# A log-space scan for the turned units, seven products for one more pair, and a new order of steps

## The chip, the cores and the metric

The kernel runs on one core of a Trainium2 chip. A core has a matrix engine (PE, with its weight loads shown apart as PEld), three engines for elementwise work (DVE, ACT and POOL), a queue engine (SP) that issues most transfers, and 16 DMA engines behind it. Each engine works through its own instructions in order and waits on semaphores for the others. The metric is the time of one execution on the device in microseconds, as the median of several executions.

## The reference

Two blocks follow one another, for 4 batches of 768 positions. In the first, 8 heads of 48 channels each keep a 48 x 48 state that decays per channel:

```python
f = 1.0 / (1.0 + np.exp(-f_logit))
for t in range(S):
    state = f[:, :, t, :, None] * state + np.einsum('bhd,bhe->bhde', k[:, :, t], v[:, :, t])
    y[:, :, t] = np.einsum('bhd,bhde->bhe', q[:, :, t], state)
```

The heads' outputs side by side are x, of 768 x 384 per batch. The second block mixes positions through a rank of 32 and channels through a hidden layer of 1536:

```python
h = xt @ U @ V                  # xt: x with positions last
u = x + h.transpose(0, 2, 1)
ch = np.maximum(u @ w_ch1, 0.0) @ w_ch2
out = u + ch
```

## The kernel before

**Units.** Two heads of one batch are a unit; there are 16, numbered 0 to 15, four per batch. A unit's 768 positions are cut into 12 chunks of 64. For a unit the kernel needs, per channel and position, the decay from a position to its chunk's end (the tile `late`, called X) and the inverse decay from the chunk's start (called Y). The keys are multiplied by X and the queries by Y. Then PE makes five groups of small products: `kept` (turns the scaled keys, tile pt), `states` (each chunk's contribution, tile ds), `scores` (within a chunk, tile sc), `read` (queries against the state, tile y) and `inner` (scores against v, added to the same y). A scan on DVE (L1111) carries the state from chunk to chunk.

**Three ways to X and Y.** Units 0 to 3 take the logarithm of the decay on ACT, sum it with a matrix product and take the exponential. Units 4 and 5 turn f on PE, take a sigmoid on ACT (`gates`, L923) and run two multiplying scans on DVE, one backwards for X (`keep`, L936) and one forwards for Y (`read`, L954, called `read_back` in the order of steps), with four small DVE instructions between them (L941 to L946). Units 6 to 15 (from `TURNED` on) do the same, but f, k and q are loaded in blocks and turned by DVE (L814), and the sigmoid is L931.

**The mixer.** For each batch, `low_rank`, `added_up` and `mix` make u; `turn` turns it (tile uT); then three pairs of position blocks go through the hidden layer. The first layer, `ch1`, makes six products per pair (tile pz, L339), each followed by a relu on ACT (L374). The second layer of batch 0, `ch2`, multiplies a pair in eight quarters (tile po, L394). The batches after it use `seven`: seven products of half the width in place of eight (tile pw, L428), by sums of blocks of w_ch2 that `quarters` makes once (four DVE subtractions, L610 to L613) and sums of the hidden layer's blocks (`sums_of`, four DVE instructions per pair). Batches 2 and 3 use `fewer` for the first layer: 15 products in place of 18, by sums of rows of w_ch1 (tile pp, L536).

**The weights.** The 24 blocks of w_ch1 and w_ch2 arrive as doubles. Each is loaded raw (L97), split by two ACT instructions (`halves`, L106 and L107), rounded by three DVE instructions (`join`, L113 to L115) and put together by one POOL addition (L116). From the seventh block on the raw data go into four buffers (`RAW`), so a load waits until a block loaded earlier has been joined.

**What sets the order.** PE's order is the program's in the whole kernel. From the start until the first two `ch1` products of batch 1, DVE's and ACT's are too, and SP's until `written.close()`. In this first part the order is that of the code: `steps` gives out the pieces of the attention, `Fill` puts pieces of the mixer between them, each weight's `end` follows a `ch1` product. After it, the pieces are collected in a list and run in the order of `ORDER2`, which permutes their 243 numbers; there a scheduler orders the engines other than PE.

**Memory between engines.** PE's results go to five PSUM tiles: three of two banks (`ps_big`: transposes, ds, sc, y, mixer sums) and two of one bank (`ps_mm`: pz, po, most pw). A tile is taken again when its last reader is done.

Of the kernel before, what the change touches and what calls it, by code (L numbers as in the profile page):

```python
# [18 lines left out]
WP = 384  # L19

RAW = 4
# [4 lines left out]

ORDER2 = (
# [44 lines left out]
SIGNS = (1, -1, 1, 1, 1, 1)  # L72


def weight_loader(nc, pool, dma):
# [8 lines left out]
    def load(dst, w, place=None):  # L84
# [25 lines left out]
        def join():  # L110
            y, r, hi = T["parts"]
            f = y.bitcast(F32)
            nc.vector.tensor_scalar(f, f, SMALLEST, LARGEST, ALU.max, ALU.min)  # L113
# [4 lines left out]
        def end():  # L118
            halves()
            join()  # L120
# [17 lines left out]
def RUN(piece):  # L138
    if TODO is None:
        return piece()  # L140
    TODO.extend(getattr(piece, "parts", (piece,)))


def of_parts(*parts):
    def run():
        for f in parts:
            f()

    run.parts = [p for f in parts for p in getattr(f, "parts", (f,))]
    return run  # L150
# [44 lines left out]
class Mixer:  # L195
# [6 lines left out]
    def __init__(self, tc, b, x, U, V, w1, w2, sums, ident, blocks, out, two, three, zp, ps_big, ps_mm, wide=False,  # L202
# [23 lines left out]
        def low_rank():  # L226
            pm = ps_mm.tile([P, 512], F32, name="ph", tag="mm")

            products_with_u(pm, slice(0, DM))
            h[0] = two.tile([P, DM], F32, name="h", bufs=2)  # L230
            nc.scalar.copy(h[0], pm[:, 0:DM])

        def added_up():

            pm = ps_mm.tile([P, 512], F32, name="ph", tag="mm")
            nc.tensor.matmul(pm[:, 0:DM], lhsT=blocks, rhs=h[0], start=True, stop=True)
            h[1] = two.tile([P, DM], F32, name="h", bufs=2)
            nc.scalar.copy(h[1], pm[:, 0:DM])
# [8 lines left out]
        def mix(t):  # L247

            s = t % 2
            if s == 0:  # L250
                pu[0] = ps_big.tile([P, 2, 512], F32, name="pu", tag="big")
            g = slice((t % NG) * R, (t % NG + 1) * R)
            nc.tensor.matmul(pu[0][:, s, 0:DM], lhsT=V[g, t // NG, :], rhs=h[1][g, :], start=True, stop=True)
            if s == 1:
                add(x[:, t - 1 : t + 1, :], x[:, t - 1 : t + 1, :], pu[0][:, :, 0:DM], ALU.add)


# [4 lines left out]
        def mix_four():  # L262
            big = ps_big.tile([P, 2, 512], F32, name="pu", tag="big")
# [4 lines left out]
            for t in range(2, NG):  # L268
                add(x[:, t, :], x[:, t, :], pms[t][:, 0:DM], ALU.add)
# [1498 lines left out]
```

## Time and profile before

| | us |
|---|---|
| median of 3 runs | 465.59 (465.1 to 465.73) |
| the profiled execution's own time | 465.49 |
| its span | 463.8 |
| PE busy | 454.1 |
| PE weight loads busy | 394.9 |
| DVE busy | 363.0 |
| ACT busy | 171.9 |
| POOL busy | 49.5 |

The span runs from the first to the last instruction of one execution; 1.7 us of the execution's time lie around it. An engine's busy time is the time in which at least one of its instructions runs. Matmuls overlap one another, and the profile models their ends, so PE can be shown busy while it works below its full pace; the starts of its instructions show the pace. A matrix product in float32 appears as two instructions. Lines such as L339 are lines of the kernel.

### The profile page before, as it was taken

What the parts mean: (1) busy time and instruction counts of PE and PEld (TensorE: products, weight loads), DVE (VectorE), ACT (ScalarE), POOL (GpSimd) and SP (SyncE); (2) the same over time, 40 slices, a digit from 0 to 9 for tenths busy, and PEclk for the clock granted to TensorE, in tenths of its full rate; (3) what the DMA queues carried; (4) which work ended last, traced back from release to release, by engine and by line L of the source; (5) the groups of instructions that cost most, each with busy time, mean ns of one, the idle gap of its engine ahead of it and who ended that gap; (6) DMA issues with size and microseconds to landing.
All of it is one profiled execution on the core that took longest, in us unless ns stands there. A gap on an engine that the chain in (4) does not pass through costs nothing.

```text
span 463.8 us, 13155 instructions
## 1 busy us (share of the span) xinstructions
PE 454.1 (98%) x5687; PEld 394.9 (85%) x5687; DVE 363.0 (78%) x614; ACT 171.9 (37%) x325; POOL 49.5 (11%) x58
## 2 busy tenths in 40 slices
PE   8999999999999999999999999999999999999997
PEld 5876888876666578899988889999989999999996
DVE  6668688988999689677799895879797974878652
ACT  6765776644332135234413542241212311212200
POOL 2002345544110101011000000000000000000000
PEclk9999999999999999999999999999999999999999
DMA  9948997678778814662406100000000100000001
GB/s 193 191 106 211 228 205 175 157 132 111 111 113 120 127 21 55 90 90 28 86 1 112 29 3 11 29 1 1 17 19 1 36 0 18 18 1 35 1 35 40
DMA packets 148584, 34.37 MB, mean 74 GB/s; under 512 B 136934, under 2 KB 146982, under 8 KB 148518
## 3 DMA queue, kind: packets, MB, share of 16 engines
q1 hardware_dynamic: 147718, 33.29, 37.2%
q8 instruction: 47, 0.77, 0.7%
q10 hardware_dynamic: 800, 0.15, 0.2%
q14 instruction: 19, 0.16, 0.1%
HBM read 28.70 MB, written 4.72 MB: 72 GB/s over the span
## 4 chain that ended last, share of the span: by engine, by line
PE 84%; DVE 7%; SPq 2%; ACT 2%; issue 2%; DMA 2%; POOL 0%; DVEq 0%; ACTq 0%; POOLq 0%
PE pw L428 27%; PE pz L339 18%; PE pp L536 18%; PE po L394 5%; PE y L1129 2%; SPq L721 2%; PE sc L1035 2%; PE y L1147 2%; PE ds L1086 2%; PE pt L1062 1%; DVE late L936 1%; PE put L327 1%; PE pt L837 1%; PE pt L895 1%; DMA w<-in_q_dram 1%
## 5 line engine op out<-in xcount | busy, mean ns | idle before, releaser
L339 PE MATMUL pz<-uT,w 128*128 128x256 f32 x420 | 96.4, 383 | 0.1
L339 PEld LDWEIGHTS pz<-uT,w 128*128 128x128 f32 x420 | 77.9, 190 | 10.9 <-ACT uT L328 0.3
L428 PE MATMUL pw<-w,z_all 128*128 128x192 f32 x216 | 37.7, 328 | 0.0
L428 PE MATMUL pw<-zw,w_raw 128*128 128x192 f32 x216 | 37.6, 328 | 0.0
L428 PEld LDWEIGHTS pw<-w,z_all 128*128 128x128 f32 x216 | 35.1, 190 | 0.9 <-DVE qT L243 0.5
L428 PEld LDWEIGHTS pw<-zw,w_raw 128*128 128x128 f32 x216 | 35.2, 190 | 0.5 <-issue 0.3
L116 POOL TENSOR_TENSOR w<-w_y,w_r 128x384 int32<-128x384 int32 x24 | 31.5, 1312 | 36.9 <-DVE w_y L115 22.5
L526 ACT ACTIVATE other<-other 128x512 f32<-128x512 f32 x18 | 11.4, 631 | 44.2 <-DVE other L243 44.2
L526 ACT ACTIVATE z_all<-z_all 128x512 f32<-128x512 f32 x18 | 11.3, 630 | 40.4 <-DVE z_all L243 40.4
L936 DVE TENSOR_TENSOR_SCAN late<-fz,late 128x768 f32<-128x768 f32 x12 | 21.1, 1754 | 6.6 <-ACT fz L931 6.5
L374 ACT ACTIVATE z_all<-pz 128x512 f32<-128x512 f32 x27 | 16.1, 597 | 26.9 <-PE pz L339 26.5
L394 PE MATMUL po<-w,zw 128*128 128x384 f32 x72 | 25.1, 495 | 0.0
L394 PE MATMUL po<-w,z_all 128*128 128x384 f32 x72 | 24.7, 493 | 0.0
L536 PE MATMUL pp<-v_nat,late 128*128 128x128 f32 x168 | 21.6, 276 | 0.0
L394 PEld LDWEIGHTS po<-w,zw 128*128 128x128 f32 x72 | 13.2, 190 | 9.6 <-issue 0.8
L1117 POOL COPY st<-added 128x576 f32<-128x576 f32 x8 | 12.5, 1560 | 81.0 <-DVE added L1111 64.6
L954 DVE TENSOR_TENSOR_SCAN late<-fz,other 128x768 f32<-128x768 f32 x12 | 21.0, 1748 | 0.1
L394 PEld LDWEIGHTS po<-w,z_all 128*128 128x128 f32 x72 | 13.3, 190 | 8.9 <-DVE o L243 0.6
L536 PEld LDWEIGHTS pp<-v_nat,late 128*128 128x128 f32 x168 | 20.2, 192 | 0.1
L1094 ACT COPY added<-ds 48x576 f32<-48x576 f32 (+2 forms) x29 | 17.8, 619 | 5.8 <-PE ds L1086 5.4
L536 PE MATMUL pp<-uT,late 128*128 128x128 f32 x144 | 19.3, 277 | 0.0
L113 DVE TENSOR_SCALAR w_y<-w_y 128x384 f32<-128x384 f32 (+3 forms) x27 | 12.1, 448 | 8.9 <-ACT w_y L106 8.9
(219 smaller groups left out, 908.4 us busy)
## 6 DMA issues: line engine op xcount, KB each, us to landing
w_raw<-in_moe_w_ch_dram SPq DMA_DIRECT2D x18, 384.0 KB, 3.8
out_dram<-o SPq DMA_DIRECT2D x17, 192.0 KB, 1.9
v_nat<-in_v_dram SPq DMA_DIRECT2D x16, 144.0 KB, 3.5
v_nat<-in_v_dram SPq DMA_DIRECT2D x32, 72.0 KB, 3.6
zw<-in_moe_w_ch_dram SPq DMA_DIRECT2D x6, 384.0 KB, 4.5
out_dram<-o SPq DMA_DIRECT2D x14, 96.0 KB, 2.2
w<-in_k_dram SPq DMA_DIRECT2D x4, 288.0 KB, 3.9
w<-in_q_dram SPq DMA_DIRECT2D x4, 288.0 KB, 4.3
```

The costliest lines, as they stand in the source:

```text
L113: nc.vector.tensor_scalar(f, f, SMALLEST, LARGEST, ALU.max, ALU.min)
L116: nc.gpsimd.tensor_tensor(dst.bitcast(I32), shaped(y.bitcast(I32)), shaped(r), ALU.add)
L339: nc.tensor.matmul(pm[:, i * 2 * P : (i + 1) * 2 * P], lhsT=w1[:, m, o : o + P], rhs=uT[a][:, m, :], start=(m == 0), stop=(m == NDC - 1))
L374: nc.scalar.activation(z[a, c][:, k : k + 2, :].rearrange("p i t -> p (i t)"), pm, AF.Relu)
L394: nc.tensor.matmul(pm, lhsT=z[a, i // NI][:, i % NI, s * P : (s + 1) * P], rhs=w2[:, i, :], start=(i == 0), stop=(i == NFC - 1))
L428: nc.tensor.matmul(W["pm"][:, n * HM : (n + 1) * HM], lhsT=lhs[:, i, :], rhs=rhs[:, i, :], start=(i == 0), stop=(i == NI - 1))
L526: nc.scalar.activation(dst, dst, AF.Relu, scale=float(SIGNS[n]))
L536: nc.tensor.matmul(pm[:, i, r * P : (r + 1) * P], lhsT=room["w"](wn)[:, r * P : (r + 1) * P], rhs=x_node(a, xn), start=((xn, wn) == of[0]) ...
L936: nc.vector.tensor_tensor_scan(backwards(X, S - 1, S), backwards(f, S, S), backwards(ends, S - 1, S), 0.0, ALU.mult, ALU.add,)
L954: nc.vector.tensor_tensor_scan(Y, f[:, 0:S], starts, 0.0, ALU.mult, ALU.add)
L1094: nc.scalar.copy(added[r, 1:].rearrange("p (e c s) -> p e c s", c=NBL, s=2)[:, e], ds[r, :, 0 : NBL * D].rearrange("p s (c e) -> p e c s", ...
L1117: nc.gpsimd.tensor_copy(st, states.rearrange(by_e, c=NCH))
```

## The change

There are three parts.

**Units 6 to 15 in logarithms.** `TURNED` units no longer use a sigmoid. POOL limits the raw f from below (`bound`), DVE turns it straight into `fz` (`gates`), ACT takes the exponential and then the logarithm of one plus it, both in one function table (`logs`), one backward scan on DVE sums the logarithms within each chunk (`keep`), and three ACT exponentials give X and the chunk's whole decay (`decay`) and Y (`read_back`). The second scan and the four small DVE instructions are gone for these units. Unit 6 has a third load of ACT's function table before it. Outside units 4 and 5 the copy into `wholes` (L917, L946) goes, since `least` holds the same numbers; `whole` is one constant tile whose first column stays zero.

**The first batch's third pair by `seven`.** The eight `ch2` quarters of pair 2 of batch 0 become seven half-width products with their sums. The four sums of w_ch2 are made earlier, between the products of pairs 0 and 1; the third of them goes into rows of `late` that the units no longer need, in two instructions. Two tiles instead of three are taken for these sums; the freed one holds two of the later sums of w_ch1.

**The order of steps.** Each piece is cut into named parts (a product `p`, the copy or sum that follows it, each transfer), and the first part of the kernel is run in the order of a table of names, `ORDER`, of 524 parts. Up to `close` it keeps the order that the code had. `ORDER2` is replaced by a permutation of 430 parts.

```diff
+        def bound_all():
...
+            nc.gpsimd.tensor_single_scalar(r["f"], r["f"], FLOOR, ALU.max)
+
+        def logs_of(i):
+            g = f[:, 0:S]
+            if i == 0:
+                if n == TURNED:
+                    nc.scalar.preload_act_table_set("natural_log_exp_and_others")
+                nc.scalar.activation(g, g, AF.Exp, scale=-1.0)
+            else:
+                nc.scalar.activation(g, g, AF.Ln, bias=1.0)
+
+        def log_scan():
+            g = f[:, 0:S]
+            nc.vector.tensor_tensor_scan(
+                backwards(g, S - 1, S), backwards(starts, S - 1, S), backwards(g, S - 1, S), 0.0, ALU.mult, ALU.add,
+            )
+
+        def decay_x():
+            X, g = late[:, 4, :], f[:, 0:S]
+            T["X"] = X
+            nc.scalar.activation(by_chunk(X)[:, :, 0 : C - 1], by_chunk(g)[:, :, 1:C], AF.Exp, scale=-1.0)
...
         def read():
             Y = T["Y"] = late[:, 5, :]
+            if n >= TURNED:
+                nc.scalar.activation(by_chunk(Y)[:, :, 0 : C - 1], by_chunk(f[:, 0:S])[:, :, 1:C], AF.Exp)
+                return
             nc.vector.tensor_tensor_scan(Y, f[:, 0:S], starts, 0.0, ALU.mult, ALU.add)
...
         def second(a):
-            if sums is None:
-                return [(2 * NFC * DM // NQ, lambda s=s, n=n: ch2(a, s, n)) for s in range(2) for n in range(NQ)]
...
+            if sums is None or wide and a < NA - 1:
+                return [(2 * NFC * DM // NQ, ch2(a, s, n)) for s in range(2) for n in range(NQ)]
```

Three stretches of `ORDER` of which the prediction speaks (names of weights, `end_w`, carry the block's number; `.t` and `.p` are products on PE):

```diff
+c.10 c.11 c.12 end_w6.halves end_w6.join load_w18 tb.m0.t load_w21 tb.m0.o end_w7.halves m0.t end_w7.join m0.o
+load_w17 c.02 m0.ch1.1.0p m0.ch1.1.0r end_w8.halves m0.ch1.2.0p end_w8.join fz1b load_w20 end_w9.halves fz0b
...
+read_back4 m0.ch1.2.2p m0.ch1.1.2r end_w15.halves queries4.f end_w15.join keys4.f m0.ch1.2.2r kept4.t
+m0.ch1.0.3p end_w16.halves end_w17.halves end_w17.join end_w16.join gates5.t m0.ch1.1.3p m0.ch1.0.3r gates5.s
+gates5.f keys5.t m0.ch1.2.3p m0.ch1.1.3r end_w18.halves kept4.o kept4.s queries4.m end_w19.halves end_w18.join
...
+m0.sv.2.01p queries9.f keys9.m scan8.s0 m0.sv.2.0e keys9.f m1.p m0.sv.2.10p m1.o m1.p#2 m1.o#2 m1.p2 logs10.e
```

More of the change, by code (lines that the diff above doesn't have):

```diff
@@ L279, in __init__ @@
+        mix_four = of_parts(("p4", mix_four_p), *[(f"f{t}", lambda t=t: mix_four_a(t)) for t in [0] + list(range(2, NG))])
+        first = 0
+        todo = []
+        if b > 1 and sums is not None:
+            todo += mix_four.parts
+            first = NG
+        for t in range(first, NCH):
+            todo += mix(t)
+        mix_blocks = of_parts(*todo)
         hs, last = {}, {}
         def low_rank_of(cols):
-            pm = ps_mm.tile([P, 512], F32, name="ph", tag="mm")
-            products_with_u(pm, cols)
@@ L284, in low_rank_of, with products @@
[L284 to L292 removed]
+            t = {}
+            def products():
+                t["pm"] = ps_mm.tile([P, 512], F32, name="ph", tag="mm")
+                products_with_u(t["pm"], cols)
@@ new lines, in put, with put_all, lo, lw @@
+        def put(label, piece):
+            todo.extend(tagged(label, piece).parts)
+        def put_all(pieces):
+            for piece in pieces:
+                RUN(piece)
+        def lo(n, *names):
+            load(n, *names)
+        def lw(i):
+            put(f"load_w{i}", weights[i][0])
+        for i in range(3):
+            put(f"busy{i}", lambda: busy(1))
+        put_all(front(0, "gates", "unpack_k", "unpack_q", "read_back", "keep"))
+        lo(1, "k", "q")
+        lo(2, "f")
@@ L1329, in factored_path @@
[L1329 to L1340 removed]
+        for i in range(FIRST, FIRST + 4):
+            lw(early + i)
```

825 lines of the change are left out of this document (505 added, 320 removed), and 31 rows, old and new, of the table ORDER2.

## The prediction

> **What bounds the kernel now.** I read the busy times first, then PE's by stage.
>
> ```profile
> PE 454.1 (98%) x5687; PEld 394.9 (85%) x5687; DVE 363.0 (78%) x614; ACT 171.9 (37%) x325; POOL 49.5 (11%) x58
> ```
>
> ```profile
> 20.00:40.00 20.00, 17.25 (x542) 14.27 (x532) 13.42 (x27) 13.44 (x35) 1.49 (x3) 1.00 0.53 139
> 80.00:100.00 20.00, 20.00 (x196) 17.20 (x196) 19.03 (x30) 12.04 (x24) 11.33 (x8) 1.00 0.71 159
> 120.00:140.00 20.00, 19.77 (x352) 13.01 (x351) 18.86 (x25) 7.42 (x13) 2.43 (x2) 1.00 0.74 110
> 280.00:300.00 20.00, 20.00 (x317) 19.55 (x316) 14.27 (x36) 5.56 (x10) 0.00 (x0) 1.00 0.06 23
> ```
>
> The columns are PE, PEld, DVE, ACT, POOL, then clock, DMA share and GB/s. PE idles in the start (17.25 of 20) and hardly after it, and its clock is full. DVE comes within 1.2 us of full between 80 and 140 us (19.03 and 18.86 of 20). So time is won or lost in two ways: PE's own work, and what makes PE wait before 140 us. For that I read PE's timeline there (start, length, line, in brackets idle time before).
>
> ```profile
> 104.83 0.84 PE L1129 MATMUL y<-st,qT 48*64 48x48 f32 x42
> 106.21 4.41 PE L394 MATMUL po<-w,zw 128*128 128x384 f32 x12
> 116.69 0.90 PE L1129 MATMUL y<-st,qT 48*64 48x48 f32 x44
> 118.16 0.76 PE L1086 MATMUL ds<-v_nat,kb 64*48 64x48 f32 x48 [0.56 <-issue]
> 118.84 4.14 PE L394 MATMUL po<-w,zw 128*128 128x384 f32 x12
> 136.35 0.59 PE L1062 MATMUL pt<-ident,kz 64*128 64x64 f32 x12 [0.23 <-DVE kz L865]
> ```
>
> The read and states products of one unit take 106.21 - 104.83 = 1.38 us, those of the next 118.84 - 116.69 = 2.15: 0.77 lost. Twelve po take 4.41 instead of 4.14: 0.27. The turn of the keys waits 0.23. Together 1.3 us of waits, all that I find after 50 us that a better order could remove.
>
> **Seven products for a pair.** The third pair's eight quarters are 48 instructions, the seven products 7 x 12 = 84. From the chain of waits (start, length):
>
> ```profile
> 69.99 2.59 PE pz L339 x12
> 73.10 2.79 PE pz L339 x12
> 136.94 7.94 PE po L394 x24
> 174.97 0.69 PE ds L1086 x48
> 178.44 0.83 PE y L1129 x44
> 436.93 23.42 PE pw L428 x144
> ```
>
> A pw costs 23.42/144 = 0.1626 us, 84 of them 13.66. Twelve pz take 2.59 us next to other full-size products and 2.79 between groups of small ones: a visit to small products costs 0.20 of the large ones' time. So 24 po without it take 7.74, 48 take 15.48, and the product saves **1.8 us** of PE. The DVE work that it adds (four sums and seven additions more) lies in 130 to 165 us, where DVE is relieved of more than that by the next part; without that cover the sums would hold the third of the seven products up. The four sums of w_ch2 are the same work, earlier.
>
> **The log scan.** These are instructions of one unit on DVE, and the next unit's first.
>
> ```profile
> 117.97 0.97 DVE L814 STREAM_TRANSPOSE late<-other 128x768 f32<-128x768 f32 x1
> 119.84 1.76 DVE L936 TENSOR_TENSOR_SCAN late<-fz,late 128x768 f32<-128x768 f32 x1 [0.90 <-ACT fz L931]
> 121.63 0.17 DVE L941 COPY least<-late 128x12 f32<-128x12 f32 x1
> 122.10 0.98 DVE L814 STREAM_TRANSPOSE kz<-other 128x768 f32<-128x768 f32 x1
> 126.57 1.75 DVE L954 TENSOR_TENSOR_SCAN late<-fz,other 128x768 f32<-128x768 f32 x1
> 130.10 0.97 DVE L814 STREAM_TRANSPOSE late<-late 128x768 f32<-128x768 f32 x1
> ```
>
> From turn to turn of f DVE needs 130.10 - 117.97 = 12.1 us per unit. It loses the second scan (1.7) and the small four (122.10 - 121.63 = 0.5): 9.9 us. ACT gets four passes for one sigmoid (0.80 for unit 5's, quoted below), 2.4 us more per unit on 7.42 of 20. PE waits for neither after 140 us, so the ten units bring nothing but the waits above: **-1.3 us**. Bounds: 0 and -1.6. What they cost is length: from f to X there is one more engine (POOL) and two more passes. The `bound` pass is not in the trace; by the nearest POOL rows it costs 1.0 (two copies of 384 columns) to 2.0 (twice an addition of 1.00, next but one fence):
>
> ```profile
> L574 POOL COPY zw<-x 128x384 f32<-128x384 f32 x2 | 1.0, 510 | 12.6 <-DVE x L243 12.6
> ```
>
> I take 1.3, nearer to the copy since it has one input too. It stands a unit ahead of its use, under some 9 us of PE work; without that cover it would cost its length once, at unit 6. The third load of ACT's table falls to ACT while DVE joins the last weights.
>
> Where POOL and DVE meet, the trace shows DVE waiting:
>
> ```profile
> 76.43 0.36 DVE L114 TENSOR_SCALAR w_y<-w_y 128x384 uint32<-128x384 uint32 x1
> 77.52 1.00 POOL L116 TENSOR_TENSOR w<-w_y,w_r 128x384 int32<-128x384 int32 x1 [1.34 <-ACT w_r L107]
> 77.69 1.04 DVE L114 TENSOR_SCALAR w_y<-w_y 128x384 uint32<-128x384 uint32 x1
> ```
>
> The same instruction takes 0.36 alone and 1.04 beside a POOL addition. The Trainium skill, SBUF — State Buffer, section "SBUF: two separate sides", says that the two engines share a port pair which is locked for a whole instruction, and that the later one waits fully. By that page each `bound` could hold DVE up for its length, and if DVE lost 1.3 us at each unit, over half of the 2.2 gained would go; the sum below would be up to 1.3 higher, as the waits would stay.
>
> **The order: more visits.** PE's sequence can be counted from `ORDER` and, numbering the parts as the code appends them, from `ORDER2`. Between the first turn of unit 4's keys and the last turn of batch 3's x, PE leaves the large products 41 times before and 52 times after. First and last in the trace:
>
> ```profile
> 72.51 0.58 PE L1062 MATMUL pt<-ident,kz 64*128 64x64 f32 x12
> 368.32 0.59 PE L327 MATMUL put<-ident,x 64*128 64x64 f32 x12
> ```
>
> Eleven visits more at 0.20 are +2.2. Small groups cost more alone, too: y takes 0.83 alone (178.44) and ds 0.69 (174.97), 1.52 in all, against 1.38 joined. Twenty such joins become fifteen: +0.7. Together **+2.9 us**. Bounds: +1.5, if half of it is hidden, and +3.5.
>
> **The order: a weight that comes late.** A raw weight's load starts when an earlier block's join ends:
>
> ```profile
> 71.45 0.35 SPq L97 DMA_DIRECT2D w_raw<-in_moe_w_ch_dram  x1
> 74.48 0.56 DVE L115 SCALAR_TENSOR_TENSOR w_y<-w_raw,w_y 128x384 uint32<-128x384 uint32 x1
> 75.11 0.33 SPq L97 DMA_DIRECT2D w_raw<-in_moe_w_ch_dram  x1
> ```
>
> ```profile
> w_raw<-in_moe_w_ch_dram SPq DMA_DIRECT2D x18, 384.0 KB, 3.8
> ```
>
> In `ORDER` blocks 18 and 21 are loaded before 17, so block 17 takes the place of the load at 75.11, after block 15's join. It lands at 75.1 + 3.8 = 78.9. ACT then has its two halves (0.54 for one, quoted next, and as much for the other), the relu of `m0.ch1.0.3` (0.60) and only then the sigmoid of unit 5 (0.80): 78.9 + 1.08 + 0.60 + 0.80 = 81.4, or some 81.2 since neighbours on ACT overlap. `keys5.t` on PE needs a two-bank PSUM tile; the three hold queries4 (freed by DVE behind two joins), kept4 (copied by ACT later) and gates5, which this sigmoid frees.
>
> ```profile
> 49.69 7.97 PE pz L339 x36
> 57.66 0.66 PE pt L837 x6
> 85.50 0.54 ACT L106 ACTIVATE w_y<-w_raw 128x384 f32<-128x384 f32 x1
> L374 ACT ACTIVATE z_all<-pz 128x512 f32<-128x512 f32 x27 | 16.1, 597 | 26.9 <-PE pz L339 26.5
> 77.41 0.80 ACT L923 ACTIVATE fz<-pt 128x756 f32<-128x756 f32 x1
> ```
>
> PE gets there after ten products of 2.59, four turns of 0.66 and one visit of 0.7: 49.7 + 25.9 + 2.6 + 0.7 = 78.9. It waits up to 2.3 us; I take **+1.5**, since DVE's joins can run a little earlier. Behind it on PE stand the pair's `ch1` products, and behind block 17's join on DVE, idle for some 4 us from block 15's, queries4, the last weights and unit 6's chain: what is left of it is late at `kept6`, where PE arrives some 34 us later and DVE's work up to unit 6's keys adds up to 33. I take **+1.0** (0 to 2.5). A third wait is in the mixer of batch 1: `m1.p2` follows `m1.p#2` at once and needs its copy by ACT, which took 0.48 and is now covered by twelve po:
>
> ```profile
> 156.87 0.48 ACT L238 COPY h<-ph 128x384 f32<-128x384 f32 x1 [4.20 <-PE ph L236]
> ```
>
> That is **+0.5**. The new waits are +3.0 (0 to 5). On SP the transfers of k and q for units 6 and 7 now stand behind the last weights' loads; their uses on DVE stand behind the last joins too, so I give them nothing, and if one is late, `kept6` is, as in (3) below.
>
> **The start.** L917 (0.20 on ACT for each of four units) goes; where ACT sets the end, in two of them, and with one visit fewer around 46 us, I take **-0.4** (0 to -0.8).
>
> ```profile
> 14.91 0.20 ACT L917 COPY whole<-least 128x11 f32<-128x11 f32 x1
> ```
>
> The sum is -1.8 - 1.3 + 2.9 + 3.0 - 0.4 = **+2.4 us**. On the profiled execution's 465.49 that is 467.9; the median lies 0.1 higher, so **468.0 us**.
>
> **Rivals.** (1) *The late weight does not reach PE.* If block 17 lands before 77 us, or ACT is earlier, the +1.5 and +1.0 go, and part of the visits is hidden (+1.5): -1.8 - 1.3 + 1.5 + 0.5 - 0.4 = -1.5, **464.1 us**, faster. For it: ACT is busy for 12.04 of 20 us only; against it: the three tiles and ACT's fixed order. (2) *Gains and costs cancel*: a third of the new waits (+1.0) and the start at its best (-0.8) make -1.8 - 1.3 + 2.9 + 1.0 - 0.8 = 0, 465.6. For it: each wait is a difference of two long sums; against it: two of the three waits follow from the order alone. (3) *DVE stays behind.* If the 4 us that DVE idles are not made up and POOL's `bound` takes more of it, the old waits stay (no -1.3) and `kept6` waits 2.5: 468.0 + 1.3 + 1.5 = **470.8**. For it: 19.03 of 20 us on DVE there now; against it: 2.2 us less per unit after. (4) *The log scan's gain is larger than its stage shows*: if PE's pace in 100 to 140 us, not only its waits, hangs on DVE's 12.1 us per unit, four units gain up to 0.5 each beyond (1): 464.1 - 2.0 = 462.1. The twelve po at 4.14, the same as at other places, speak against it.
>
> **Chances.** The forecast 0.47, (1) 0.25, (2) 0.12, (3) 0.10, (4) 0.06. A difference under 0.2%, 0.93 us, can't be told from none here. Faster is (1) and (4): 0.31; same is (2) with the edges of the others: 0.15; slower 0.54. The range runs from 463.2, into (1) and short of (4), to 470.8; the forecast's own is 466.6 to 469.8.
>
> **What would show it.** In the profile after: 84 pw around 150 us for the last 48 po; a wait of PE at the turn of unit 5's keys near 79 us that ends with ACT's sigmoid; block 17's load right after block 15's join; waits of 0.2 to 0.8 us no longer at L1086; DVE under 17 of 20 us in 120 to 140; PE at 20.00 of 20 from 180 us on with pz groups of 12 at 2.79. If PE passes 79 us without a wait, or the whole after 180 us is shorter than before, the forecast is wrong.

## The result and the profile after

The changed kernel takes 470.72 us as the median of six executions (469.15 to 474.02); the kernel before, beside it on the same chip, 465.08 (464.9 to 465.73). The ratio is 1.0127 with a 95% interval of 1.0088 to 1.0166: slower by 5.6 us. The profiled execution took 470.39 us with a span of 468.7, 4.9 more than the 463.8 before. The forecast was 468.0, with a range from 463.2 to 470.8.

The busy times of the profile after, and some stages of 20 us (PE, PEld, DVE, ACT, POOL, then clock, DMA share and GB/s):

```profile
PE 455.9 (97%) x5723; PEld 399.0 (85%) x5723; DVE 350.7 (75%) x580; ACT 194.5 (42%) x353; POOL 71.5 (15%) x67
```

```profile
80.00:100.00 20.00, 19.03 (x146) 16.24 (x145) 18.55 (x32) 12.32 (x24) 11.47 (x8) 1.00 0.74 170
100.00:120.00 20.00, 18.20 (x292) 11.85 (x290) 17.62 (x27) 13.21 (x22) 10.18 (x7) 1.00 0.78 105
120.00:140.00 20.00, 20.00 (x360) 12.69 (x362) 16.36 (x19) 8.69 (x16) 4.76 (x2) 1.00 0.79 120
140.00:160.00 20.00, 19.43 (x317) 13.76 (x308) 17.59 (x18) 9.83 (x17) 7.39 (x4) 1.00 0.53 83
```

DVE was relieved by 12 us, ACT and POOL got 23 and 22 more, and PE has the 36 instructions more that 84 pw for 48 po are. The waits of before lay near 118 and 136 us; between 115 and 140 us PE now stands nowhere. It stands before and after that. These are all the waits of PE's timeline after 50 us, in brackets the wait and what ended it:

```profile
79.37 0.87 PE L1020 MATMUL pt<-ident,other 128*128 128x128 f32 x6 [0.44 <-ACT f L1141]
87.08 8.04 PE L463 MATMUL pz<-uT,w 128*128 128x256 f32 x36 [0.97 <-ACT zw L508]
114.18 0.59 PE L1322 MATMUL pt<-ident,kz 64*128 64x64 f32 x12 [1.80 <-DVE kz L1066]
159.29 0.92 PE L327 MATMUL pu<-h,V 32*128 32x384 f32 x6 [0.57 <-ACT h L308]
...
347.61 0.91 PE L327 MATMUL pu<-h,V 32*128 32x384 f32 x4 [0.41 <-DVE x L315]
```

The first is the turn of unit 5's keys behind its sigmoid, the third the turn of unit 6's scaled keys (`kept6`), the fourth `m1.p2`. The second, a first-layer product that waits for a relu on ACT, and the last were not in the forecast. And PE often visits its small products one group at a time; three rows of the same timeline:

```profile
101.61 0.93 PE L1296 MATMUL sc<-qT,kz 48*64 48x64 f32 x48
102.46 2.20 PE L529 MATMUL po<-w,z_all 128*128 128x384 f32 x6
104.60 0.76 PE L1344 MATMUL ds<-v_nat,kb 64*48 64x48 f32 x48
```

Worked out from the starts of all of PE's instructions, the 4.9 us are these, beside the forecast's terms (the start is the time up to the first turn of unit 4's keys, 72.51 us before and 72.31 after):

| term | forecast | in the trace |
|---|---|---|
| 84 pw for 48 po | -1.8 | -1.8 |
| waits of the kernel before that are gone | -1.3 | -1.3 |
| 11 visits more (41 to 52) at 0.20 | +2.2 | +2.2 |
| small products apart that were joined | +0.7 | +1.8 |
| new waits after 50 us | +3.0 | +4.2 |
| start | -0.4 | -0.2 |
| sum | +2.4 | +4.9 |

The new waits are the five rows above. The visits are counted as in the forecast; the texts of the experiments count 60 for the same kernel, since they take the 128 x 128 turns and one full-size mixer product for small ones too. The medians differ by 0.7 more than the two profiled executions; the section on the clock comes back to it.

### The profile page after: what moved, and what is told of

The parts are those of the page before. It is cut to its first block, busy times and chain, and to the rows that moved or that the text cites. A ratio compares the mean times of both kernels' runs of the same rounds, so it can differ in the third digit from the quotient of the medians.

```text
span 468.7 us, 13242 instructions
## 1 busy us (share of the span) xinstructions
PE 455.9 (97%) x5723; PEld 399.0 (85%) x5723; DVE 350.7 (75%) x580; ACT 194.5 (42%) x353; POOL 71.5 (15%) x67
## 4 chain that ended last, share of the span: by engine, by line
PE 86%; DVE 5%; DMA 2%; SPq 2%; ACT 2%; issue 2%; DVEq 0%; ACTq 0%
PE pw L574 29%; PE pz L463 17%; PE pp L691 16%; PE po L529 5%; PE y L1392 3%; PE sc L1296 2%; PE y L1411 2%; PE ds L1344 2%; SPq L900 2%; DMA w_raw<-in_moe_w_ch_dram 2%; PE pt L1322 2%; PE pt L1103 1%; PE put L446 1%; PE pt L1020 1%; PE pu L327 1%
## 5 line engine op out<-in xcount | busy, mean ns | idle before, releaser
L574 PE MATMUL pw<-zw,w_raw 128*128 128x192 f32 x168 | 30.1, 329 | 0.0
L574 PEld LDWEIGHTS pw<-zw,w_raw 128*128 128x128 f32 x168 | 27.3, 190 | 0.8 <-DVE kz L1066 0.3
L1167 DVE TENSOR_TENSOR_SCAN fz<-other,fz 128x768 f32<-128x768 f32 x10 | 17.6, 1757 | 8.5 <-ACT fz L1163 8.5
L1380 POOL COPY st<-added 128x576 f32<-128x576 f32 x8 | 11.5, 1435 | 69.4 <-DVE added L1370 56.2
L1370 DVE TENSOR_TENSOR_SCAN added<-added,whole 128x576 f32<-128x576 f32 x12 | 16.2, 1353 | 4.7 <-ACT added L1353 4.7
L1308 DVE TENSOR_TENSOR A<-sc,causal 128x768 f32<-128x768 f32 x16 | 15.2, 948 | 5.1 <-PE sc L1296 5.1
L574 PE MATMUL pw<-w,other 128*128 128x192 f32 x108 | 18.5, 326 | 0.0
L315 DVE TENSOR_TENSOR w_raw<-z_all 128x768 f32<-128x768 f32 x13 | 13.3, 1027 | 6.8 <-ACT z_all L508 5.6
L1392 PEld LDWEIGHTS y<-st,qT 48*64 48x64 f32 x704 | 13.6, 137 | 5.2 <-issue 3.4
L574 PEld LDWEIGHTS pw<-w,other 128*128 128x128 f32 x108 | 17.4, 190 | 0.0
L529 PE MATMUL po<-w,zw 128*128 128x384 f32 x48 | 17.1, 499 | 0.0
```

Source lines behind the costliest of these rows:

```text
L315: nc.vector.tensor_tensor(*args)
L529: nc.tensor.matmul(pm, lhsT=z[a, i // NI][:, i % NI, s * P : (s + 1) * P], rhs=w2[:, i, :], start=(i == 0), stop=(i == NFC - 1))
L574: nc.tensor.matmul(W["pm"][:, n * HM : (n + 1) * HM], lhsT=lhs[:, i, :], rhs=rhs[:, i, :], start=(i == 0), stop=(i == NI - 1))
L1167: nc.vector.tensor_tensor_scan(backwards(g, S - 1, S), backwards(starts, S - 1, S), backwards(g, S - 1, S), 0.0, ALU.mult, ALU.add,)
L1370: nc.vector.tensor_tensor_scan(states[:, of], added[:, of], whole.rearrange("p e c -> p (e c)")[:, of], 0.0, ALU.add, ALU.mult)
L1392: nc.tensor.matmul(o(c % 2, par, c // 2), lhsT=T["q"][rows[par], chunk[c]], rhs=T["st"][rows[par], c, :], start=(c <= 2), stop=False, skip ...
```

## The experiments

Two theories stood against each other. A: the order is the loss, by its late weight and its visits. B: the log scan and the seven products are the loss, in any order.

**The late weight.** `ORDER` loads blocks 18 and 21 ahead of block 17. SP's queue, and POOL's timeline with the joins and unit 6's bound (L1154), of the kernel after:

```profile
73.20 0.33 SPq L166 DMA_DIRECT2D w_raw<-in_moe_w_ch_dram  x1
```

```profile
73.27 1.00 POOL L186 TENSOR_TENSOR w<-w_y,w_r 128x384 int32<-128x384 int32 x1 [1.34 <-ACT z_all L508]
77.44 2.13 POOL L1154 TENSOR_SCALAR late<-late 128x768 f32<-128x768 f32 x1 [3.17 <-DMA late<-in_q_dram]
79.62 1.01 POOL L186 TENSOR_TENSOR w<-w_y,w_r 128x384 int32<-128x384 int32 x1
```

Block 17's load is issued at 73.20, right after block 15's join on DVE, and for 6.3 us no addition of a block begins on POOL. In `e_loads` the loads follow the numbers:

```diff
-c.10 c.11 c.12 end_w6.halves end_w6.join load_w18 tb.m0.t load_w21 tb.m0.o end_w7.halves m0.t end_w7.join m0.o
-load_w17 c.02 m0.ch1.1.0p m0.ch1.1.0r end_w8.halves m0.ch1.2.0p end_w8.join fz1b load_w20 end_w9.halves fz0b
...
+c.10 c.11 c.12 end_w6.halves end_w6.join load_w17 tb.m0.t load_w18 tb.m0.o end_w7.halves m0.t end_w7.join m0.o
+load_w19 c.02 m0.ch1.1.0p m0.ch1.1.0r end_w8.halves m0.ch1.2.0p end_w8.join fz1b load_w20 end_w9.halves fz0b
...
-end_w13.join end_w14.halves keys4.t load_w25 load_w26 keys4.m load_w24 m0.ch1.0.2r m0.ch1.1.2p end_w14.join
+end_w13.join end_w14.halves keys4.t load_w24 load_w25 keys4.m load_w26 m0.ch1.0.2r m0.ch1.1.2p end_w14.join
```

> The changed kernel with the loads of the w_ch1/w_ch2 blocks in the order of their numbers (in ORDER: 17, 18, 20, 19 for 18, 21, 17, 20; 24, 25, 26 for 25, 26, 24), nothing else moved. Theory A1 (the late weight): the gap of POOL's joins between 73.3 and 79.6 us closes, PE's waits at the turn of unit 5's keys (0.44) and for the relu at 86.1 (0.97) go, the stream of weights ends 1.5 us earlier and the wait at unit 6's k (1.80) falls to 0.5: -2.7, 467.7 us. Theory A2 (the wait at unit 6 is its own chain, table load, two passes and scan): 0.44 and 0.97 go, 1.80 stays: 469.0. Theory A3 (ACT's and DVE's other work sets these waits): 470.4, nothing moves.

(The places of 18, 21, 17, 20 and 19 got 17, 18, 19, 20 and 21; the text has its third and fourth number the wrong way round.)

Measured: 467.65 us (467.27 to 468.63), ratio to the kernel before 1.0060 (1.0042 to 1.0077). Its PE and POOL timelines:

```profile
112.33 0.59 PE L1322 MATMUL pt<-ident,kz 64*128 64x64 f32 x12 [1.39 <-DVE kz L1066]
```

```profile
73.47 1.00 POOL L186 TENSOR_TENSOR w<-w_y,w_r 128x384 int32<-128x384 int32 x1 [1.34 <-DMA late<-in_f_logit_dram]
76.58 1.00 POOL L186 TENSOR_TENSOR w<-w_y,w_r 128x384 int32<-128x384 int32 x1 [2.10 <-issue]
```

The gap is 3.1 us, the waits of 0.44 and 0.97 are gone, the one at `kept6` is 1.39. A1's total is right, its share at `kept6` is not: most of that wait stays, as A2 had it. The spans of the profiled executions differ by 1.9 (468.7 to 466.8), the medians by 3.1. What is left of the wait shows in the kernel after, on ACT (the third table load, then the two passes) and on DVE (the join of the last weight but one, then further on the mask, the turn of k and the scan):

```profile
105.83 1.28 ACT L1160 ACT_TABLE_LOAD   x1
108.00 0.85 ACT L1163 ACTIVATE fz<-fz 128x768 f32<-128x768 f32 x1
```

```profile
105.40 0.36 DVE L183 TENSOR_SCALAR w_y<-w_y 128x384 f32<-128x384 f32 x1 [1.75 <-ACT w_y L175]
...
108.62 0.95 DVE L1308 TENSOR_TENSOR A<-sc,causal 128x768 f32<-128x768 f32 x1
109.48 0.97 DVE L995 STREAM_TRANSPOSE kz<-late 128x768 f32<-128x768 f32 x1
110.38 1.80 DVE L1167 TENSOR_TENSOR_SCAN fz<-other,fz 128x768 f32<-128x768 f32 x1
```

The logarithm is ready at 108.85, the scan begins at 110.38, behind the joins of the last two weights, a mask and a turn that stand ahead of it. In these joins DVE itself stands for 1.75 us, for a weight's halves from ACT. If DVE's sequence is the limit, an earlier table load gives nothing. `e_table`:

```diff
+            if n + 1 == TURNED:      # behind unit 5's second sigmoid
+                nc.scalar.preload_act_table_set("natural_log_exp_and_others")
```

> The changed kernel with ACT's third table load (1.28 us, at 105.83) put behind the last sigmoid (unit 5's, at 79.1). Theory A2 (unit 6's chain on ACT sets the wait at its k): the exponential starts 1.3 us earlier and the wait of 1.80 falls to about 0.5: 469.1 us. Theory A1 (DVE, behind the last weights, sets it: its scan starts at 110.38 although the logarithm is ready at 108.85, since the joins, a mask and a turn of k stand ahead of it): no change, 470.4 us, the scan still starts at about 110.4.

Measured: 471.42 us (469.24 to 473.09), ratio 1.0126 (1.0081 to 1.0171), and PE waits 1.84 at the same place. The logarithm is now ready at 107.69, and the scan still begins only at 110.65. So DVE's sequence sets this wait, not the table load or the two passes. How much of it the last two joins make was not tried: no run takes them out of the scan's way.

**The parts by themselves.** `e_quarters` takes the seven products back. Its last quarters read a part of w_ch2 that the fourth sum has overwritten; the instructions are the same.

```diff
-            if sums is None or wide and a < NA - 1:
+            if sums is None or wide:
```

> The changed kernel with the third pair of batch 0 by eight quarters of ch2 again, at the places of the seven products; its sums go. If the seven products save what PE's rows say (48 po at 0.3227 are 15.49, 84 pw at 0.1625 are 13.65): +1.8, 472.2 us. If the DVE work that they bring (four sums, seven additions) or their tiles hold PE up: less than that, 470.4 us or under.

Measured: 473.03 us (472.6 to 473.19), 2.3 more than the kernel after. The spans differ by 2.8 (468.7 to 471.5). New waits are in it, 0.60 for that fourth sum and 0.29 for an addition, which leave 1.4 of the medians' difference and 1.9 of the spans'. In PE's own rows, without the waits, the second layer's po and pw take 2.2 us more. The forecast's 1.8 lies among these, so the products' saving stands.

`e_logscan` puts the log scan alone into the kernel before:

```diff
-            nc.scalar.activation(by_chunk[:, :, 1:C], fv[:, :, 1:C], AF.Sigmoid)
+            nc.scalar.activation(f[:, 0:S], f[:, 0:S], AF.Exp, scale=-1.0)
+            nc.scalar.activation(f[:, 0:S], f[:, 0:S], AF.Ln, bias=1.0)
...
+            if TURNED <= n + 1 < NU:
+                bound(n + 1, raw[(n + 1) % 2])      # on POOL, in the step of q
```

> The kernel before with the log scan alone for units 6 to 15 (bound on POOL one unit ahead, inside the step of q; the third load of the table; the copy into wholes stays), its quarters for the third pair and its own order. Theory A (the log scan only relieves DVE, so PE's waits of the order before go): -1.3 us on the kernel before (between 0 and -1.6), 463.7 us, with PE's visits as before. Theory B (the chain from f to X, longer by one engine and two passes, is a loss in any order): new waits of PE at the turns of k of units 6 to 9, 466 us or more.

Measured: 468.05 us (467.39 to 471.15), ratio 1.0078 (1.0053 to 1.0103): a loss of 3.1, where A had a gain of 1.3. B's time is right and its place is wrong. PE's waits after 50 us (but for one of 0.15), and POOL's and ACT's rows before the first of them:

```profile
109.99 0.91 PE L394 MATMUL po<-w,zw 128*128 128x384 f32 x2 [1.30 <-POOL w L116]
146.00 0.91 PE L1169 MATMUL y<-v_nat,A 64*64 64x48 f32 x48 [0.41 <-ACT seen L1158]
...
206.65 4.17 PE L428 MATMUL pw<-zw,w_raw 128*128 128x192 f32 x24 [1.30 <-ACT z_all L374]
```

```profile
104.10 2.13 POOL L940 TENSOR_SCALAR other<-other 128x768 f32<-128x768 f32 x1
107.62 2.31 POOL L116 TENSOR_TENSOR w<-w_y,w_r 128x384 int32<-128x384 int32 x1 [1.39 <-DVE w_y L115]
```

```profile
101.58 1.28 ACT L930 ACT_TABLE_LOAD   x1
103.93 0.85 ACT L931 ACTIVATE fz<-fz 128x768 f32<-128x768 f32 x1 [1.07 <-DVE fz L814]
...
105.56 0.54 ACT L106 ACTIVATE w_y<-w_raw 128x384 f32<-128x384 f32 x1
```

The old waits (0.56, 0.23 and the pause between the read and states products) are gone, as said. In their place PE waits for the last weight's join, and twice for ACT, which has the two passes more. POOL had ended its bound at 106.23 and stood 1.39 us before that join began. On ACT the third table load and the two passes stand ahead of this weight's halves (105.56). To see whether POOL's bound ahead of the join matters, `e_log_dve` makes it on DVE:

```diff
-            nc.gpsimd.tensor_single_scalar(r["f"], r["f"], FLOOR, ALU.max)
+            nc.vector.tensor_single_scalar(r["f"], r["f"], FLOOR, ALU.max)
```

> The log scan alone in the kernel before (468.05 us), with its lower bound on DVE instead of POOL. Theory A (the bound's 2.1 us on POOL ahead of the last weight's join make PE wait 1.30 at 110 us): that wait goes, 466.7 us. Theory B (the loss is ACT's two more passes and the longer chain, the place of the bound is one symptom): 467.6 us or more, with DVE's work per unit longer by the bound.

Measured: 467.40 us (467.08 to 468.19), ratio 1.0062 (1.0049 to 1.0075). The wait for the join is still 1.17, though POOL now stands for 3.48 us before it; the halves of this weight are again behind the table load and the two passes (105.55). The three waits for ACT's `seen` are 0.28, 0.55 and 0.75, and one of 0.40 for an addition on DVE has come. So theory A fails: the bound on POOL does not make this wait, and the time is nearer to B's. The two medians lie 0.6 apart with overlapping intervals, so what the bound's place is worth is not shown to differ from nothing.

**The code's own order.** `e_default` drops both tables; the parts run as the code makes them.

```diff
-        todo = [(l, by[l]) for l in ORDER]
```

> The changed kernel with both tables taken out: its parts run in the order in which the code makes them; log scan and the seven products stay. PE's list then has 47 visits to small products instead of 60, and 85 groups of small products instead of 89. Theory A (the order is the loss): 13 visits of 0.20 us and four joins of 0.14 come back (-3.2), and the waits of the profile after that belong to its order go (0.44 + 0.97 + 1.80 + 0.57 + 0.41 = 4.2): 470.4 - 7.4 = 463.0 us, or 464.3 if the waits of the order before (1.3) are back. Theory B (the log scan is the loss: one more engine and two more passes between f and X make PE wait in any order): the visits come back, the waits do not, 467.2 us or more, with waits of PE at the turn of k for units 6 to 9.

Measured: 478.75 us (477.15 to 480.79), ratio 1.0292 (1.0248 to 1.0336). Theory A fails: with 47 visits it is the slowest of all. B's time (467.2 or more) is met, but none of the largest waits stands at a turn of k. Its largest waits of PE (total, times, longest):

```profile
PE pu L326 <- DVE x L314: 3.0, 1, 3.0
PE y L1410 <- ACT seen L1399: 2.6, 2, 2.3
PE pw L573 <- ACT z_all L507: 2.4, 1, 2.4
```

So the tables do not only lose; against the code's order they win 8 us. Its thirteen visits fewer are outweighed by its waits, which add up to 11.5 us after 50 us.

**Fewer visits.** Where can visits be joined without waits? `e_attend` has the loads in order and joins units 4 to 8's products between 100 and 152 us:

```diff
+m0.ch2.0.00p scores4.p scores4.m states5.p read4.p
...
+m0.ch2.0.10p kept6.t scores5.p
...
+read6.p read6.s states7.p
...
+inner6.p kept8.t
...
+m0.ch2.1.13p scores7.p states8.p read7.p
```

> The changed kernel with the loads in order (467.65 us) and units 4 to 8's small products joined between 100 and 152 us (55 visits on PE's list instead of 60); the turn of unit 6's k has one more po group ahead of it. Theory A: -1.0 (five visits of 0.20) - 0.7 (five joins of 0.14) - 1.4 (the wait at unit 6's k) = -3.1, 464.5 us. Theory B (the searched order kept these products apart because their inputs come one by one): waits inside the joined visits (for st, for ACT's seen, for a free tile of PSUM) take it back, 467 us or more.

Measured: 466.42 us (465.26 to 467.10), ratio 1.0033 (1.0012 to 1.0053): 1.2 won, not 3.1. In its timeline the wait at `kept6` is nearly gone (0.15), and a new one stands behind the last joined visit:

```profile
145.29 2.22 PE L574 MATMUL pw<-w,z_all 128*128 128x192 f32 x12 [1.18 <-DVE A L1308]
```

Scores, states and read hold all three two-bank PSUM tiles there, and the pair's first product needs one (in batch 0 the seven products take such tiles).

`e_late` leaves `ORDER` at the loads in order and moves eight products in `ORDER2`, after 180 us. There the edit changes numbers; these are the parts that they stand for, at their new places:

```text
kept10.t scores9.p inner8.p inner8.o
...
kept11.t inner9.p
...
read10.p scores11.p scores11.m
...
read11.p read11.s states12.p
...
m2.mf.p4 m2.mx.p4 m2.mx.p5
...
m2.turn0.t m2.turn0.o scores12.p
...
m2.turn1.t m2.turn1.o read12.p
...
scores14.p scores14.m read14.p
```

> The changed kernel with the loads in order (467.65 us) and, in ORDER2 alone, eight small products moved into a neighbour's visit (53 visits on PE's list instead of 60); ORDER stays. Theory A (a visit costs its 0.20 wherever DVE is not behind): -1.4 - 0.7 (joins) = -2.1, 465.5 us, and no new wait of PE after 180 us. Theory B (the visits of this stage are hidden or their joins wait): 467.6.

Measured: 466.08 us (465.16 to 468.01), ratio 1.0030 (1.0016 to 1.0045): 1.6 for seven visits, close to A's 2.1; A's condition of no new wait is not met, since one of 0.39 stands behind the joined mixer products of batch 2. `e_best1` has both, with unit 7's read taken out of its joined visit again:

> The kernel e_attend (466.42 us) with the read of unit 7 taken out of the joined visit, where the product after it waited 1.18 for a third PSUM tile, and with the eight moves of ORDER2: 466.4 - 1.2 + 0.3 - 2.1 = 463.4 us, faster than the kernel before by 0.3%. If the searched order's own visits bought something there: 465 us or more.

Measured: 464.60 us (464.20 to 465.24), ratio 0.9997 (0.9988 to 1.0007): level with the kernel before, at 41 visits after 50 us in the trace, as many as there. Its waits up to 240 us, but for one of 0.23 at `kept6`:

```profile
141.72 0.76 PE L1343 MATMUL ds<-v_nat,kb 64*48 64x48 f32 x48 [0.81 <-ACT kb L1326]
155.05 0.92 PE L326 MATMUL pu<-h,V 32*128 32x384 f32 x6 [0.57 <-ACT h L307]
```

Three edits went for these. `e_best4` turns unit 8's k one po group earlier (`kept8.t` ahead of `m0.ch2.1.11p`), `e_best6` also puts batch 3's last mixer products later, `e_best2` puts `scores8.p` between `m1.p#2` and `m1.p2`.

> The kernel e_best1 (464.60 us) with the turn of unit 8's k one po group earlier, so that its copy (PE waited 0.81 for it) has two groups of cover: 463.8 us. If k of unit 8 is not ready then (it is ready some 1 us before its turn now): the wait only moves, 464.6.

> The kernel e_best4 with the last two mixer products of batch 3 one group of products later, where PE waited 0.41 for DVE's addition: 463.8 - 0.4 = 463.4 us, faster than the kernel before (464.78) by 0.3%. If its end of the mixer is late then: 463.8.

> The same kernel with the scores of unit 8 put between m1.p#2 and m1.p2, so that they cover the copy that m1.p2 waits for (0.57), and one visit fewer: 463.4 - 0.8 = 462.6 us. If DVE, which gets the mask of unit 8 among the additions of this stage, holds PSUM tiles longer by it: 463.4 or more, with a wait of PE at the next products for DVE.

Measured: 464.68 us (ratio 1.0005, 0.9997 to 1.0014), 464.82 (1.0002, 0.9992 to 1.0012) and 467.42 (1.0058, 1.0038 to 1.0078). In `e_best4` the wait of 0.81 becomes one of 0.85 at the next pw, for the mask A, so it only moved; in `e_best6` the wait of 0.41 stands at a pp product instead, for the same addition; `e_best2` loses the wait of 0.57 and gets waits of 0.99 for a relu at 199 us and 0.85 for an addition at 220.

**The joined mixer.** `e_mixer` (loads in order) has batch 1's six mixer products in one visit, as the kernel before had them:

```diff
+m0.sv.2.11p m1.p0 m1.p1 m1.a1 m1.p2 m1.p3 m1.a3 m1.p4 m1.p5 m1.a5
...
+m0.sv.2.21p m1.t scores8.p
```

> The changed kernel with the loads in order (467.65 us) and the mixer of batch 1 as in the kernel before: its six products in one visit, twelve pw later; the turn of pair 0 and the scores of unit 8 share a visit. PE's list has 58 visits instead of 60. Theory A (each visit costs 0.20, each group of two mixer products alone some 0.35 more, and the wait of 0.57 for the copy goes): -0.4 - 0.7 - 0.6 = -1.7, 465.9 us. Theory B (the three PSUM tiles and DVE's additions set this stage's pace): waits of the same sum at the next turn, 467.6.

Measured: 474.15 us (473.63 to 474.96), ratio 1.0199 (1.0148 to 1.0249): 6.5 lost where 1.7 were to be won. PE's longest wait, DVE's waits before it, and POOL's rows:

```profile
169.60 3.33 PE L574 MATMUL pw<-w,w_raw 128*128 128x192 f32 x12 [2.93 <-DVE w_y L315]
```

```profile
159.26 1.82 DVE L315 TENSOR_TENSOR x<-x,pu 128x768 f32<-128x768 f32 x2 [3.92 <-PE pu L327]
165.39 0.98 DVE L995 STREAM_TRANSPOSE fz<-other 128x768 f32<-128x768 f32 x1 [2.56 <-POOL other L1154]
```

```profile
162.31 0.96 POOL L729 COPY zw<-x 128x384 f32<-128x384 f32 x2 [6.25 <-DVE x L315]
163.24 2.12 POOL L1154 TENSOR_SCALAR other<-other 128x768 f32<-128x768 f32 x1
```

DVE stands for the mixer's first product, then for unit 11's bound, which POOL runs behind two copies of the mixer; the seven products' additions are queued behind both, and PE waits for one of them, with the clock at half for 3.4 us behind it (the section on the clock). Unit 11's turn stands in `ORDER2`, and DVE takes it ahead of parts of `ORDER`: in this stretch DVE's order is not the table's (the section on the kernel before has DVE in the program's order up to there). `e_visits` is `e_mixer`, `e_attend` and `e_late` together; `e_psum` is `e_visits` with the seven products of batch 0 in one-bank tiles:

```diff
-                if (room["last"] == a - pair) if room else (a == NA - 1 - kept):
+                if (room["last"] == a - pair) if room else (b and a == NA - 1 - kept):
```

> The two edits before this together, and in ORDER2 eight more small products moved into a neighbour's visit (46 visits on PE's list instead of 60). Theory A: -2.8 (14 visits) - 0.7 (mixer products) - 1.0 (some seven joins of 0.14) - 0.6 - 1.4 (the two waits) = -6.5 on 467.65: 461.2 us, faster than the kernel before. Theory B: waits in the joined visits take back half or more: 464.5 us or more.

> The kernel e_visits (470.25 us, joined mixer products) with the seven products of batch 0 in the one-bank PSUM tiles instead of the two-bank tiles that they share with the attention and the mixer. Theory C (the loss of the joined mixer, 2.9 + 1.4 + 0.9, and the 1.18 behind the joined read of unit 7 are waits for the three two-bank tiles): about 464 us. Theory D (DVE's work, the seven products' additions ahead of the mixer's, sets them whatever the tile): 469 us or more.

Measured: 470.25 us (ratio 1.0108, 1.0059 to 1.0157) and 469.26 (1.0101, 1.0078 to 1.0124). The tiles give back 1.0 at most; in `e_psum` PE waits 1.83, 1.50 and 1.73 for DVE's additions and mask, theory D. Then the bound on DVE, in `e_mixer` and in `e_best1` with the joined mixer:

> The kernel e_mixer (474.15 us) with the lower bound of the raw f on DVE instead of POOL. In e_mixer DVE stood 2.56 us for unit 11's bound, which POOL ran behind two copies of the mixer, and the seven products' additions stood behind it; PE waited 2.93 for one of them. Theory A (POOL's place in the chain is that loss): both waits go, 471.2 us or less. Theory B (the joined mixer products themselves hold DVE up, which waits 3.92 for the first of them): 473.5 us or more, with PE's wait still ended by DVE's w_y.

> The kernel e_best1 (464.60 us) with the joined mixer of batch 1 and the lower bound on DVE (47 visits on PE's list). If the bound on POOL was what made the joined mixer dear: 464.6 - 1.7 (two visits, the mixer's groups, the wait of 0.57) + 0.3 (DVE's longer units) = 463.2 us, faster than the kernel before by 0.3%. If the joined mixer is dear in itself: 467 us or more.

Measured: 471.78 us (469.81 to 472.90; ratio 1.0148, 1.0120 to 1.0175) and 467.70 (466.52 to 468.71; 1.0064, 1.0047 to 1.0081). In `e_mixer_dve`:

```profile
169.01 2.19 PE L574 MATMUL pw<-w,w_raw 128*128 128x192 f32 x12 [0.93 <-DVE w_y L315]
```

```profile
160.66 1.82 DVE L315 TENSOR_TENSOR x<-x,pu 128x768 f32<-128x768 f32 x2 [4.08 <-PE pu L327]
...
163.77 0.86 DVE L1154 TENSOR_SCALAR other<-other 128x768 f32<-128x768 f32 x1
```

The wait for POOL is gone, and 2.0 of PE's 2.93 with it; DVE's wait for the first mixer product stays, with 0.93 of PE's. The time lies between the two theories, nearer to A's. So POOL's bound is a good part of that loss. `e_all_dve` still loses 3.1 against `e_best1`, but not by the mixer alone: the bound on DVE has its price too, since the wait at `kept6` grows from 0.23 to 1.01. At the mixer and behind it PE waits 1.04 and 0.93, and later 1.06 and 0.67, where `e_best1` has 0.57 and 0.39.

**The clock.** `e_wait` is `e_loads` with one memset of DVE ahead of unit 6's chain made three times.

```diff
-                nc.vector.memset(starts, 1.0)
+                for _ in range(3):
+                    nc.vector.memset(starts, 1.0)
```

> The changed kernel with the loads in order (467.65 us), with one memset of DVE ahead of unit 6's chain done three times instead of once (twice 0.70 us, same values). Theory A (a wait of PE past some 1.8 us also lowers the granted clock for the work behind it): the wait at the turn of unit 6's k grows from 1.39 to 2.8, and behind it a group of 12 po takes more than 4.14 us in most executions: 467.65 + 1.4 + 1.4 = 470.4 us, with a mean clock under 1.0. Theory B (a wait costs its own length): 469.0 us, clock 1.0.

Measured: 471.91 us (470.80 to 473.06), ratio 1.0148 (1.0129 to 1.0167), mean clock 0.993 to 0.996 in all four executions. PE's timeline and one microsecond of it:

```profile
113.74 0.77 PE L1323 MATMUL pt<-ident,kz 64*128 64x64 f32 x12 [3.25 <-DVE kz L1066]
114.44 1.56 PE L1297 MATMUL sc<-qT,kz 48*64 48x64 f32 x48
...
117.18 5.91 PE L529 MATMUL po<-w,z_all 128*128 128x384 f32 x12
```

```profile
114.00:115.00 1.00, 1.00 (x31) 0.88 (x30) 1.00 (x1) 0.98 (x3) 0.00 (x0) 0.50 0.98 121
```

The wait is 1.9 longer than in `e_loads` and the kernel 4.3 slower. Behind the wait the granted clock reads 0.50 in each microsecond from 114 to 120, 0.60 in the next, then 1.00: some 6.8 us at half. Twelve po take 5.91 us (4.14 elsewhere) and the scores 1.56 (0.93): theory A. The same stands in `e_table`, behind a wait hardly longer than that of the profiled execution after:

```profile
114.45 0.59 PE L1322 MATMUL pt<-ident,kz 64*128 64x64 f32 x12 [1.84 <-DVE kz L1066]
...
116.77 5.54 PE L529 MATMUL po<-w,z_all 128*128 128x384 f32 x12
```

There the clock reads 0.61, 0.50, 0.50 and 0.68 in the four microseconds from 116 on, which is half the clock for 3.4 us, and po and the small products take some 1.6 us more than in the kernel after. Such a stretch lowers the mean clock of an execution to 0.996 (3.4 x 0.5 of some 470 us).

In the profiles a stretch at half stands behind the waits of 3.25, 3.01, 2.93 (in two runs), 2.43, 2.34 and 1.84, and behind one of 1.83 with another of 1.50 close after it (`e_psum`). None stands behind the waits of 2.27 (`e_mixer_dve`), 1.80 (the kernel after), 1.79 (`e_quarters`) and 1.73 (`e_psum`), or behind a single wait of up to 1.42. So from some 1.8 to 2.3 us a wait did it in some executions only.

Of the kernel after's six executions, the two slowest (472.88 and 474.02) have mean clocks of 0.996 and 0.986, the others 1.0; all six of `e_loads`, whose wait is 1.39, have 1.0. The four with 1.0 have a median of 469.84 (between 469.29 and 470.39), 2.2 above `e_loads` and 4.8 above the kernel before. So about 0.9 us of the medians' 3.1 for the loads and 5.6 for the change goes with the clock. The waits of executions without a profile are not known: in `e_late`, whose longest profiled wait after 50 us is 1.40, one of eleven has 0.996.

## Why the prediction was right or wrong

The direction was right, the size was not: 2.4 of some 5.6 us.

- **Seven products, -1.8.** Right, by the rows and by `e_quarters`.
- **The log scan, -1.3.** The waits that it was to remove are gone, but the log scan costs more than length. Alone it loses 3.1 us (`e_logscan`): ACT's table load and two passes stand ahead of the last weight's halves and make its join late, and PE waits for a relu and for `seen`, both on ACT. The bound takes 2.1 us and more, not 1.3; the nearest row was an addition made twice, not a copy. In the changed kernel its cost can't be told apart from the order's: it is within the wait at `kept6`, of which 1.39 are left when the loads are in order. What sets that rest is DVE's sequence, with the joins of the last two weights in it, not block 17's late load.
- **More visits, +2.9.** Eleven more at 0.20, as counted. The groups taken apart cost 1.8 instead of 0.7: more than half of it are the mixer's products, which the forecast did not price (12 together took 1.49 us, as 6, 2 and 4 they take 0.85 each).
- **The late weight, +1.5 and +1.0.** The mechanism was right, and mending it is the largest single gain (3.1 us in the medians, 1.9 in the profiled spans). Its sizes were off: block 17's load came at 73.2, not 75.1, so the keys of unit 5 waited 0.44; a wait for a relu (0.97) was not seen; `kept6` waited 1.80, inside its range. A wait of 0.41 for an addition of batch 3's mixer was put at nothing too.
- **`m1.p2`, +0.5.** 0.57.
- **The start, -0.4.** -0.2 in the two profiles. One profile does not tell this term: in `e_logscan`, whose code up to there is that of the kernel before, the first turn of unit 4's keys stands at 71.50 and not at 72.51.
- **What the sum left out.** Every wait was priced at its length. A stretch at half clock behind a wait of about 1.8 us adds to it in some executions: some 0.9 us of the median.

So the step that failed is the size of two terms of the sum: the new waits, +3.0, measured 4.2, and the small products taken apart, +0.7, measured 1.8. In both, the excess is of things put at nothing: the waits for the relu and for the addition, and the mixer's products. The clock behind a wait, also put at nothing, comes on top.

Of the rivals, (1) fell, since the late weight did reach PE. (3), old waits kept, named 470.8, near the measured time, by luck: the old waits went, and DVE was less busy than before from 120 to 140 us (16.36 of 20 against 18.86).

What the forecast quoted of the Trainium skill, SBUF — State Buffer, section "SBUF: two separate sides", that a bound on POOL could hold DVE up for its length, was seen only in a small part. Bounds on POOL, and an addition on DVE, in the kernel after:

```profile
109.74 2.13 POOL L1154 TENSOR_SCALAR other<-other 128x768 f32<-128x768 f32 x1
...
129.85 3.58 POOL L1154 TENSOR_SCALAR other<-other 128x768 f32<-128x768 f32 x1
...
143.44 2.85 POOL L1154 TENSOR_SCALAR late<-late 128x768 f32<-128x768 f32 x1
```

```profile
144.23 1.57 DVE L315 TENSOR_TENSOR w_raw<-z_all 128x768 f32<-128x768 f32 x1
```

Beside the first, DVE's scan at 110.38 (shown above) takes 1.80, against 1.75 at 146.59 beside no bound. The second is longer itself (3.58 against 2.13), and DVE's instructions beside it are not. Beside the third, the addition takes 1.57 where the others of its size take 0.91 to 0.95. By these rows and their like, DVE's instructions beside the ten bounds are longer by some 2 us in all, an estimate: 0.2 per unit, and not 1.3.

The kernel `e_best1` ends level with the one before, though it keeps the seven products' 1.8, and its trace says why. Behind the first turn of unit 4's keys, PE's large products take 2.3 us less than before (1.8 of it the seven products'), its waits 1.6 more (2.4 against 0.8) and its small products 0.6 more, the mixer's divided groups among them. These add up to -0.1 us.

## What to carry to other kernels

A table of steps for one engine is also an order for the loads and for the engines that feed it: look in it for a transfer ahead of one that is needed earlier, and for work ahead of the start of a long chain. Joining small products can pay (1.6 us for seven visits after 180 us) and can cost (6.5 us for two visits near 160, of which the bound on POOL made a part); ask which engine drains them and what it has in its queue there. Price a wait of PE above its length once it comes near 2 us, as a chance, and a move of work to idle engines by the chain that it lengthens, not by the busy time that it frees.

## What the runs showed of the hardware

A wait of PE can be followed by a lower granted clock. 3.25 us was, in the profile of `e_wait`: the clock read 0.50 for some 6.8 us, and twelve po took 1.8 us longer. 1.84 us was, in the profile of `e_table` (0.50 for 3.4 us, twelve po 5.54 instead of 4.14), while 2.27 and 1.80 in two others were not. The Trainium skill, TensorE: Matmul & The Clock Gate, section "Part 1: The HAM clock gate (the "warmup" mystery)", says that the clock falls to half after an idle window of about 3.4 us. The half is what the traces show. The execution of `e_table` fell after 1.84 us, so here less than a full window of that length was enough; that its windows run freely, as the Trainium skill also says there, would fit a wait that does it in some executions only, which no run here tests.

The same lower bound of 128 x 768 takes 2.13 us and more on POOL, and 0.86 (`e_mixer_dve`) or 0.56 (`e_log_dve`) on DVE. A visit of PE to small products costs the large ones around it 0.20 us, and seven visits fewer gave the 1.4 that this makes (`e_late`, large products without waits).
